# First expert weights bounded two pairs early, high part on VectorE; another order in the first pair

## The chip, the cores and the metric

The kernel runs on one core of a Trainium2 chip. The metric is the device time of one execution in microseconds (us); lower is better. On one core TensorE multiplies matrices, VectorE, ScalarE and GpSimd (POOL in the profile) work on elements, SyncE issues every load and store (SP), and 16 DMA engines carry them. TensorE writes into PSUM, which the other engines read.

## The reference

Three steps follow each other. The rows that attention gives are the rows `x` (1152 x 512) of the experts, and their sum is the input of the last step.

```
q_pool = mean of two neighbouring rows of q        # 2 batches x 8 heads, 1152 -> 576 rows, d = 64
scores = scale * q_pool @ k.T                      # 576 x 1152 a head
attn   = exp(scores - rowmax) / rowsum
x      = attn @ v                                  # gathered to 1152 x 512

p      = domain_probs / sum(domain_probs)          # 4 experts
y      = sum over e of p[:, e] * (relu(x @ w1[e]) @ w2[e])     # 512 -> 1024 -> 512

out    = ((y @ a) * (y @ b)) @ w3 @ w_out
```

## The kernel before

Every large operand is split exactly into a high and a low part, so that TensorE can work on two narrow numbers instead of a wide one: the high part is the scaled and rounded value, the low part what rounding left. To scale, the range has to be known first: a reduce over each partition, a small matmul with ones that spreads it over the partitions, and three small VectorE operations that make a power of two of it (`bounds`).

Attention goes through eight pairs of heads i = 0..7, in each two heads s, in each head nine chunks c of 128 keys. A chunk is a score product `s{i}_{s}_{c}`, two passes of ScalarE over it (exponential `p` L537, and its f16 high part `ph` L541), the low part `pl` = p - ph on GpSimd (L548) or, for the chunks named in LO_DVE and for the last pair in LAST, on VectorE (L546), and products `av` with the values `vt` (L572, L574). Beside that the next pair is prepared: keys are transposed (`kt`), their high part is made on ScalarE (`kab`) and their low part on VectorE (`kl` L263); queries are pooled on GpSimd (`QP`), transposed (`qt`) and split (`qh`, `QZ`, `ql`); `vm` (L444), `vp`, `vs` are the range of the values, and `vt` their split parts (high on ScalarE L497, low on VectorE L501). For the row maxima that the exponential subtracts, coarse score products `mp` (L367) are reduced on VectorE (`mx` L370), gathered (`mf`), turned by TensorE (`mr`) and split (`mh` on ScalarE, `ml` on VectorE L410), then laid into the operand Q2 by four small DMAs.

What runs when is an agenda: a list of (slot, function), filled with hand-written slot numbers and sorted. A pair takes 18 slots; t = 18 i. The sorted list sets the program order on each engine, and each engine works in that order. The constants at the top of the file are slots: K0, V1, VL1 for the first pair's keys and values, MX0 for the maxima, CX and CXT for the range of the rows (`cm`, `cxt`, `ca`, `cxd`, `cxs`, `cx`), W0 and WT for the weights of the experts. Score banks, `av` and two work tags (two banks and one bank) share PSUM; the work tags serve `kt`, `qt`, `mp`, `mr`, `vp`, `cxt` and `cxs` in turn, each waiting until the one before it has been read.

The clock of TensorE follows what it does, so WARM_E matmuls on an idle tile are run behind the maxima of head 0. At slot 130 the work banks are closed and three banks open for the experts: the rows are transposed (`xt` L766) and split into `xA` (high on ScalarE L783, low on VectorE L793), while the last pair still runs. The experts' weights come in 16 groups g of 256 columns. `prep_w` loads one group into two tiles `rw` of 128 x 1024, reduces them (`wm` L650), spreads and bounds them (`ws`, `wab`), and makes their high part on ScalarE (L670) and their low part on VectorE (L671). The first products `up` (L696) need `xA` and group 0.

## Time and profile before

| | us |
| --- | --- |
| median of 3 runs | 840.73 |
| runs | 839.34, 841.78, 840.73 |
| the profiled execution | 842.56 |
| its span | 840.6 |
| TensorE busy in it | 814.8 |
| VectorE, ScalarE, GpSimd busy | 602.4, 441.7, 310.6 |

The span is what the profiler saw between the first and the last instruction. A row of a timeline gives the start, the duration, the engine, the line, the operation, out<-in with shapes, how many instructions are run together (x), and in brackets the idle time of that engine before it and what ended it. Durations of matmuls that follow each other overlap.

### The profile page before, as it was taken

The page shows a single profiled execution, that of the slowest core. Times are in us where ns is not written, and L with a number is a line of the kernel's source. Part 1 is how long each engine was busy: PE and PEld are TensorE (multiplying, and loading weights), DVE is VectorE, ACT ScalarE, POOL GpSimd, SP SyncE. Part 2 cuts the span into 40 slices and gives each one's busy share as a digit, 9 for nine tenths or more (in the row PEclk, how much of TensorE's full clock was granted, in tenths as well). Part 3 has the DMA queues.
Part 4 walks back from the last instruction along what each step waited for, and adds up shares of the span by engine and source line. Part 5 has one row for each costly group of instructions (what it writes and reads, how often), then busy time and mean ns, then how long its engine had stood idle before and what let it go on. Part 6 is the DMA issues. An engine that isn't in the chain of part 4 may idle for free.

```text
span 840.6 us, 15989 instructions
## 1 busy us (share of the span) xinstructions
PE 814.8 (97%) x6367; PEld 571.4 (68%) x6367; DVE 602.4 (72%) x1025; ACT 441.7 (53%) x813; POOL 310.6 (37%) x275
## 2 busy tenths in 40 slices
PE   7789999999989999999999999999999999999998
PEld 6678889888867555555555555555556559999887
DVE  6878787887856566777788889897679778886000
ACT  2878888888775534333344445664324544433111
POOL 5788988898732000000001102221010146766100
PEclk9999999999989999999999999999999999999999
DMA  7668775774620122212232333221110222220011
GB/s 183 163 154 192 182 160 129 172 181 100 145 58 27 27 76 76 76 51 76 76 96 81 95 108 102 74 74 53 49 50 27 76 78 83 91 76 26 13 51 50
DMA packets 59834, 76.75 MB, mean 91 GB/s; under 512 B 23480, under 2 KB 41264, under 8 KB 59760
## 3 DMA queue, kind: packets, MB, share of 16 engines
q1 hardware_dynamic: 59760, 75.73, 33.9%
q8 instruction: 50, 0.82, 0.4%
q14 instruction: 24, 0.20, 0.1%
HBM read 51.92 MB, written 2.36 MB: 65 GB/s over the span
## 4 chain that ended last, share of the span: by engine, by line
PE 86%; DVE 5%; ACT 4%; DMA 2%; issue 1%; POOL 1%; SPq 0%; DVEq 0%; ACTq 0%; POOLq 0%
PE up L696 22%; PE dn L736 22%; PE gt L1210 12%; PE s L521 7%; PE o L1227 6%; PE wf L1175 5%; PE av L574 4%; PE mp L367 4%; DVE mx L370 2%; PE av L572 2%; ACT ph L541 1%; ACT p L537 1%; DMA rv<-in_v 1%; PE w3t L1162 1%; DMA Q<-qh 1%
## 5 line engine op out<-in xcount | busy, mean ns | idle before, releaser
L548 POOL TENSOR_TENSOR pl<-p,ph 128x576 f16<-128x576 f32 x131 | 169.1, 1312 | 54.9 <-ACT ph L541 50.2
L736 PE MATMUL dn<-w,h 128*128 128x512 f16 x840 | 184.7, 379 | 0.0
L696 PEld LDWEIGHTS <-w 128*128 128x128 f16 x1152 | 111.9, 98 | 77.4 <-issue 1.7
L736 PEld LDWEIGHTS <-h 128*128 128x128 f16 x840 | 81.6, 98 | 94.7
L702 ACT ACTIVATE up<-up 128x320 f32<-128x320 f32 (+1 forms) x96 | 45.7, 476 | 141.7 <-PE up L696 126.6
L370 DVE TENSOR_REDUCE mx<-mp 128x1 f32<-128x768 f32 (+1 forms) x144 | 101.9, 751 | 24.7 <-PE mp L367 24.2
L521 PE MATMUL s<-Q,K 128*128 128x288 f32 x576 | 109.9, 315 | 5.1 <-ACT ph L541 3.6
L696 PE MATMUL up<-xB,w 128*128 128x320 f16 x768 | 109.9, 299 | 0.6 <-DVE xB L793 0.5
L537 ACT ACTIVATE p<-s 128x576 f32<-128x576 f32 x131 | 84.8, 647 | 17.4 <-PE s L521 16.2
L707 DVE TENSOR_TENSOR h<-up,h 128x320 f16<-128x320 f32 (+1 forms) x94 | 51.0, 552 | 57.2 <-ACT h L703 56.9
L541 ACT ACTIVATE ph<-s 128x576 f16<-128x576 f32 x144 | 92.0, 648 | 0.0
L696 PE MATMUL up<-xA,w 128*128 128x512 f16 x384 | 90.7, 384 | 0.3 <-DVE w L671 0.3
L521 PEld LDWEIGHTS s<-Q,K 128*128 128x128 f32 x576 | 83.8, 192 | 7.1 <-ACT ph L541 4.1
L843 POOL TENSOR_TENSOR wo<-wo,cv_a 128x512 f32<-128x512 f32 x8 | 10.2, 1269 | 210.9 <-DVE wo L840 118.4
L574 PE MATMUL av<-vt,ph 128*128 128x65 f16 x720 | 80.6, 193 | 2.6 <-DVE x L584 1.5
L574 PE MATMUL av<-vt,pl 128*128 128x65 f16 x720 | 80.8, 196 | 0.0
L572 PE MATMUL av<-vt,ph 128*128 128x64 f16 x720 | 80.5, 194 | 0.0
L574 PEld LDWEIGHTS <-ph 128*128 128x128 f16 x720 | 67.1, 99 | 7.3 <-DVE x L584 3.0
L572 PEld LDWEIGHTS <-ph 128*128 128x128 f16 x720 | 66.8, 97 | 6.2 <-issue 3.3
L574 PEld LDWEIGHTS <-pl 128*128 128x128 f16 x720 | 67.0, 98 | 4.1 <-issue 1.6
L843 POOL TENSOR_TENSOR r<-r,cv_a 128x512 f32<-128x512 f32 x16 | 20.3, 1270 | 126.9 <-DVE r L840 92.1
L367 PE MATMUL mp<-kab,QZ 128*128 128x384 f32 x216 | 56.6, 369 | 1.6 <-DVE mx L370 1.3
(169 smaller groups left out, 1333.5 us busy)
## 6 DMA issues: line engine op xcount, KB each, us to landing
rw<-in_moe_w SPq DMA_DIRECT2D x64, 512.0 KB
K<-kab SPq DMA_DIRECT2D x32, 288.0 KB
rk<-in_k SPq DMA_DIRECT2D x16, 288.0 KB
rv<-in_v SPq DMA_DIRECT2D x8, 576.0 KB
Q<-qh SPq DMA_DIRECT2D x32, 144.0 KB
K<-kl SPq DMA_DIRECT2D x16, 288.0 KB
rq<-in_q SPq DMA_DIRECT2D x8, 512.0 KB
rw<-in_moe_w_out SPq DMA_DIRECT2D x8, 512.0 KB
```

The costliest lines, as they stand in the source:

```text
L367: mm(ps[:, n, :PC], QZ[:, o : o + P], KAB[i][:, sl], start=True, stop=True)
L370: nc.vector.tensor_reduce(out=mx[i, s][:, j, g : g + 1], in_=st.pop((j, g))[:, :, :PC], axis=AX.XY, op=ALU.max)
L521: mm(ps[:, n, :HALF], a[s][:, cs], b[s][:, n * HALF : (n + 1) * HALF], start=first, stop=not first,)
L537: nc.scalar.activation(out=o, in_=x, func=AF.Exp, scale=SCORE)
L541: nc.scalar.activation(out=two(o), in_=st["s"][:, :, :HALF], func=AF.Exp, scale=SCORE)
L548: nc.gpsimd.tensor_tensor(out=o, in0=st["p"], in1=h, op=ALU.subtract)
L572: mm(t[:, j, 0:D], p, vt[s][:, c, 0:D], start=False, stop=False)
L574: mm(t[:, j, :], p, vt[s][:, c, D:], start=(c == 0 and n == 0), stop=(c == NC - 1 and n == 2))
L696: mm(p, w[:, a, c, fc * P : (fc + 1) * P], x[b][:, c, lo - o : hi - o], start=(c == 0 and a == b), stop=(c == KD - 1 and a == 1),)
L707: nc.vector.tensor_tensor(out=hl[:, fc, lo:hi], in0=st["p"], in1=hh[:, fc, lo:hi], op=ALU.subtract)
L736: mm(p, hid[n][a][:, fc, t * P : (t + 1) * P], w[:, b, fc, :], start=(fc == 0 and a == b), stop=(fc == 1 and a == 1),)
L1210: mm(p, mws[n][:, m, a, c * P : (c + 1) * P], x[b][:, c, lo - o : hi - o], start=(i == 0), stop=(i == 11),)
```

## The change

Five things are changed. WARM_E goes from 27 to 45, and WARM_T adds 8 more matmuls behind the turn of head 0. In the first pair the slots K0, V1, VL1 move, Q0 and MXF are new, and so keys, queries, values and maxima stand in another order. The range of the rows (CX, CXT) is done in one go before the first maxima of pair 7's head 0 instead of between them. `prep_w` is taken apart for group 0: its load stands at slot 84 (before 123.5), its two reduces at 91.4 and 96.1, its bounds at 110.2, and its high part is made on VectorE by a tensor_scalar at 127.6 and 129.5, each followed by the low part. In the last pair chunk 4's low part goes from VectorE to GpSimd (LAST), and the split of the rows is issued later (XC).

```
--- before.py
+++ after.py
@@ -29,17 +29,18 @@
 VL0 = -4.21
 VR = 4.92
 VE = 0.35
-V1 = 4.6
-VL1 = 6.1
-K0 = 0.45
+V1 = 5.55
+VL1 = 6.3
+K0 = 1.2
+Q0 = 1.21
 L0 = (15.6, 15.7)
 LV2 = 15.8
 PQ = 1.67
 PQS = 1.3
 SH = 62.45
 XR = 120.3
-CX = 113.2
-CXT = (0, 3.4, 3.45, 5.8, 5.85)
+CX = 113.35
+CXT = (0, 0.55, 0.6, 1.25, 1.3)
 LK1 = -10
 LQ1 = -10
 LV1 = -9
@@ -48,7 +49,8 @@
 WARM = 39
 WARM_K = 10
 WARM_N = 5
-WARM_E = 27
+WARM_E = 45
+WARM_T = 8
 VH0 = 1.5
 FIRST = (0.71, 1.14, 2.3, 3.1)
 NEAR = 0.0
@@ -56,17 +58,18 @@
 KT = (3.05, 3.05)
 QT = 4.89
 MX0 = (7, 8, 10, 11.72, 13.01)
+MXF = (8, 9, 10.3, 11.72, 13.01)
 MX1 = (14, 16, 17, 18.92)
 ME = 0.07
-LAST = ((2, 4, 6), (1, 5, 7))
+LAST = ((2, 6), (1, 5, 7))
 SW = 130
-W0 = 123.5
 W1 = 134
-WT = ((0, 4.6, 8.2, 8.4, 10), (0, 7.0, 11.5, 13.0))
+WT = ((84, 91.4, 96.1, 110.2, 128.6, 127.6, 128.25, 129.5, 130.5), (0, 7.0, 11.5, 13.0))
 WN = (1, 4, 5, 3, 0)
 WS = 6
 XA = 0.0
 XS = 0.9
+XC = (0.75, 1.1)
 UA = 134
 US = 2
 DT = (139, 143.8)
@@ -419,6 +422,7 @@
         at(e, end)
         if (i, s) == (0, 0):
             at(e + TURN, turn_now)
+            at(e + TURN + 0.01, warm, WARM_T)
             return
         at(e + TURN, turn)
         at(e + TURN + 0.1, cut_hi)
@@ -629,7 +633,7 @@
 
     wab, share_of = {}, {}
 
-    def prep_w(g, space, eng=None):
+    def prep_w(g, space):
 
 
         e, o = divmod(g, PER)
@@ -644,35 +648,47 @@
                 )
                 raws.append(t)
 
-        def rows():
-            st["m"] = wtiny.tile([P, 2], BF16, tag="wm", name=f"wm{g}")
-            for m in range(2):
-                nc.vector.tensor_reduce(
-                    out=st["m"][:, m : m + 1], in_=raws[m], axis=AX.X, op=ALU.max, apply_absolute_value=True
-                )
+        def row(m):
+            if m == 0:
+                st["m"] = wtiny.tile([P, 2], BF16, tag="wm", name=f"wm{g}")
+            nc.vector.tensor_reduce(
+                out=st["m"][:, m : m + 1], in_=raws[m], axis=AX.X, op=ALU.max, apply_absolute_value=True
+            )
 
         def spread():
             p = space(f"ws{g}")
             mm(p[:, :2], ones, st["m"], start=True, stop=True)
             c = wab[g] = wtiny.tile([P, 4], F32, tag="wab", name=f"wab{g}")
             bounds(p[:, :2], c[:, 2:4], c[:, 0:2], 2.0**-100)
+
+        def share():
+            c = wab[g]
             share_of[g] = wtiny.tile([P, 9], F32, tag="sh", name=f"sh{g}")
             nc.vector.tensor_scalar(
                 out=share_of[g], in0=prx[:, :, e], scalar1=c[:, 2:3], scalar2=c[:, 3:4], op0=ALU.mult, op1=ALU.mult
             )
 
-        def cut(m):
+        def hi(m):
             if m == 0:
                 w = spl.tile([P, 2, 2, 2 * DM], F16, tag="spl", name=f"w{g}")
                 w1s[g], w2s[g] = w[:, 0], w[:, 1]
+            o, c = (w1s, w2s)[m][g][:, 0], wab[g][:, m : m + 1]
+            if g:
+                nc.scalar.activation(out=o, in_=raws[m], func=AF.Copy, scale=c)
+            else:
+                nc.vector.tensor_scalar(out=o, in0=raws[m], scalar1=c, scalar2=None, op0=ALU.mult)
+
+        def lo(m):
             w = (w1s, w2s)[m][g]
-            c = wab[g][:, m : m + 1]
-            nc.scalar.activation(out=w[:, 0], in_=raws[m], func=AF.Copy, scale=c)
-            (eng or nc.vector).scalar_tensor_tensor(
-                out=w[:, 1], in0=raws[m], scalar=c, in1=w[:, 0], op0=ALU.mult, op1=ALU.subtract
-            )
-
-        return [load, rows, spread, lambda: cut(0), lambda: cut(1)]
+            nc.vector.scalar_tensor_tensor(
+                out=w[:, 1], in0=raws[m], scalar=wab[g][:, m : m + 1], in1=w[:, 0], op0=ALU.mult, op1=ALU.subtract
+            )
+
+        steps = (load, lambda: row(0), lambda: row(1), spread, share)
+        steps += (lambda: hi(0), lambda: lo(0), lambda: hi(1), lambda: lo(1))
+        if g == 0:
+            return steps
+        return [load, lambda: run(steps[1:3]), lambda: run(steps[3:5]), lambda: run(steps[5:7]), lambda: run(steps[7:])]
 
     def up_tiles(n, space, h_tiles):
 
@@ -920,9 +936,10 @@
                 for n in range(3):
                     at(u + KT[0] - PQ + n * PQS, pool_q, i + 1, n)
                 plan_k(i + 1, u if i else u + K0)
-                plan_q(i + 1, u + QT + NEAR, u + QT + QH_)
+                q0 = 0 if i else Q0
+                plan_q(i + 1, u + QT + NEAR + q0, u + QT + QH_ + q0)
                 plan_spread(i + 1, 0, t + 9)
-                plan_max(i + 1, 0, [u + x for x in MX0])
+                plan_max(i + 1, 0, [u + x for x in (MX0 if i else MXF)])
                 plan_max(i + 1, 1, [u + x for x in MX1])
                 at((LV1, LV2)[i] if i < 2 else t + VL0, load_v, i + 1)
                 r = t + (VR if i else V1)
@@ -944,13 +961,13 @@
         later = []
 
         def plan_w(g, t, space):
-            steps = prep_w(g, space, nc.vector)
+            steps = prep_w(g, space)
             for f, d in zip(steps, WT[g]):
                 at(t + d, f)
             if g == 1:
                 later.append(steps[4])
 
-        plan_w(0, W0, one_bank)
+        plan_w(0, 0, lambda name: work(1, name)[:, 0])
         plan_w(1, W1, one_bank)
         plan_rows(CX)
         at(XR, rows_share)
@@ -961,8 +978,8 @@
         for n in range(NB):
             pe, to_hi, to_lo = rows_tile(x_src, n, one_bank, f"xt{n}", True)
             at(t + XS * n, pe)
-            at(t + XS * n + 0.2, to_hi)
-            at(t + XS * n + 0.5, to_lo)
+            at(t + XS * n + XC[0], to_hi)
+            at(t + XS * n + XC[1], to_lo)
         xb_p = []
 
         def rows_b():
```

The first pair's preparation on TensorE, before (`kt1`, `qt1`, `vp1` belong to pair 1, `mr0_1` is the turn for head 1 of pair 0):

```order
L257 MATMUL kt1_0_454<-ident_64,rk1_363 128x128 x6
L257 MATMUL kt1_1_461<-ident_64,rk1_363 128x128 x3
L521 MATMUL s0_0_4_466<-Q1_0_127,K1_0_123 128x288 x2
L521 MATMUL s0_0_4_466<-Q2_0_129,K2_0_125 128x288 x2
L310 MATMUL qt1_485<-ident_64,QP_133 128x128 x5
L448 LDWEIGHTS ones_74
L448 MATMUL vp1_491<-vm_75,ones_74 128x2
L521 MATMUL s0_0_5_497<-Q1_0_127,K1_0_123 128x288 x2
L521 MATMUL s0_0_5_497<-Q2_0_129,K2_0_125 128x288 x2
L402 MATMUL mr0_1_504<-ident_64,mf0_1_474 5x128
L521 MATMUL s0_0_6_521<-Q1_0_127,K1_0_123 128x288 x2
```

And now on TensorE in the same place of the first pair:

```order
L525 MATMUL s0_0_4_480<-Q1_0_127,K1_0_123 128x288 x2
L525 MATMUL s0_0_4_480<-Q2_0_129,K2_0_125 128x288 x2
L260 MATMUL kt1_0_492<-ident_64,rk1_390 128x128 x6
L260 MATMUL kt1_1_499<-ident_64,rk1_390 128x128 x3
L525 MATMUL s0_0_5_507<-Q1_0_127,K1_0_123 128x288 x2
L525 MATMUL s0_0_5_507<-Q2_0_129,K2_0_125 128x288 x2
L405 MATMUL mr0_1_516<-ident_64,mf0_1_486 5x128
L452 LDWEIGHTS ones_74
L452 MATMUL vp1_529<-vm_75,ones_74 128x2
L525 MATMUL s0_0_6_535<-Q1_0_127,K1_0_123 128x288 x2
L525 MATMUL s0_0_6_535<-Q2_0_129,K2_0_125 128x288 x2
L313 MATMUL qt1_543<-ident_64,QP_133 128x128 x5
```

The turn moved ahead of `vp1`, and `qt1` behind `vp1` and the chunk s0_0_6.

VectorE from the last maxima of pair 7 to the first row part, before:

```order
L370 TENSOR_REDUCE mx7_1_4314<-mp7_1_3_1_4502 128x1
L386 TENSOR_REDUCE mf7_1_4533<-mx7_1_4314 128x4
L387 TENSOR_REDUCE mf7_1_4533<-mx7_0_4118 128x1
L650 TENSOR_REDUCE wm0_4544<-rw0_0_4366 128x1
L650 TENSOR_REDUCE wm0_4544<-rw0_1_4368 128x1
L501 SCALAR_TENSOR_TENSOR vt0_121<-rv7_3693,vs7_4071,vt0_121 128x9x64
L546 TENSOR_TENSOR pl7_0_4482<-s7_0_2_4536,ph7_0_4481 128x576
L410 TENSOR_TENSOR ml7_1_4589<-mr7_1_4580,mh7_1_4584 5x128
L793 SCALAR_TENSOR_TENSOR xA1_4616<-xt0_4618,cx_77,xA0_4615 128x4x128
```

And now on VectorE in the same place:

```order
L373 TENSOR_REDUCE mx7_1_4354<-mp7_1_3_1_4538 128x1
L679 TENSOR_SCALAR w0_4562<-rw0_0_3077,wab0_3970 128x1024
L389 TENSOR_REDUCE mf7_1_4571<-mx7_1_4354 128x4
L390 TENSOR_REDUCE mf7_1_4571<-mx7_0_4170 128x1
L683 SCALAR_TENSOR_TENSOR w0_4562<-rw0_0_3077,wab0_3970,w0_4562 128x1024
L505 SCALAR_TENSOR_TENSOR vt0_121<-rv7_3727,vs7_4109,vt0_121 128x9x64
L667 TENSOR_SCALAR sh0_4599<-prx_79,wab0_3970 128x9
L550 TENSOR_TENSOR pl7_0_4518<-s7_0_2_4574,ph7_0_4517 128x576
L413 TENSOR_TENSOR ml7_1_4627<-mr7_1_4618,mh7_1_4622 5x128
L679 TENSOR_SCALAR w0_4562<-rw0_1_3079,wab0_3970 128x1024
L683 SCALAR_TENSOR_TENSOR w0_4562<-rw0_1_3079,wab0_3970,w0_4562 128x1024
L809 SCALAR_TENSOR_TENSOR xA1_4655<-xt0_4657,cx_77,xA0_4654 128x4x128
```

The two reduces `wm0` are gone from here; the high and low parts of the weights stand around `mf7_1` and `ml7_1`, all ahead of the first `xA1`.

ScalarE at the same time, from chunk 3 of pair 7's first head, before:

```order
L537 ACTIVATE p32_7_0_3_4597<-s7_0_3_4574 128x576
L541 ACTIVATE ph7_0_4481<-s7_0_3_4574 128x576
L783 ACTIVATE xA0_4615<-xt0_4618,cx_77 128x4x128
L541 ACTIVATE ph7_0_4481<-s7_0_4_4606 128x576
L537 ACTIVATE s7_0_4_4606<-s7_0_4_4606 128x2x288
L783 ACTIVATE xA0_4615<-xt1_4649,cx_77 128x4x128
L537 ACTIVATE p32_7_0_5_4679<-s7_0_5_4657 128x576
L670 ACTIVATE w0_4703<-rw0_0_4366,wab0_4688 128x1024
L783 ACTIVATE xA0_4615<-xt2_4697,cx_77 128x4x128
```

And now on ScalarE in the same place:

```order
L541 ACTIVATE p32_7_0_3_4635<-s7_0_3_4612 128x576
L545 ACTIVATE ph7_0_4517<-s7_0_3_4612 128x576
L541 ACTIVATE p32_7_0_4_4675<-s7_0_4_4645 128x576
L799 ACTIVATE xA0_4654<-xt0_4657,cx_77 128x4x128
L545 ACTIVATE ph7_0_4517<-s7_0_4_4645 128x576
L541 ACTIVATE p32_7_0_5_4718<-s7_0_5_4697 128x576
L799 ACTIVATE xA0_4654<-xt1_4689,cx_77 128x4x128
L545 ACTIVATE ph7_0_4517<-s7_0_5_4697 128x576
L545 ACTIVATE ph7_0_4517<-s7_0_6_4736 128x576
```

The two weight parts are gone, and each row part `xA0` stands behind the exponential of the next chunk.

## Rows read from the trace of the kernel before

**Rows 1.** The page, busy time by engine: us (share of the span) xinstructions

```profile
PE 814.8 (97%) x6367; PEld 571.4 (68%) x6367; DVE 602.4 (72%) x1025; ACT 441.7 (53%) x813; POOL 310.6 (37%) x275
```

**Rows 2.** Timeline of TensorE, first pair (columns as told above)

```profile
14.49 1.68 PE L874 MATMUL warm<-idle 128*128 128x128 f16 x27
17.56 0.70 PE L397 MATMUL mr<-ident,MT 128*2 128x128 f32 x5 [1.39 <-DVE MT L391]
...
30.41 0.73 PE L310 MATMUL qt<-ident,QP 128*128 128x128 f32 x5 [1.13 <-DVE kl L263]
32.05 0.18 PE L448 MATMUL vp<-vm,ones 128*128 128x2 bf16 x1 [0.90 <-DVE vm L444]
...
34.40 0.79 PE L521 MATMUL s<-Q,K 128*128 128x288 f32 x4 [0.90 <-ACT ph L541]
35.03 0.69 PE L367 MATMUL mp<-kab,QZ 128*128 128x384 f32 x3
```

**Rows 3.** Windows: from:to, us; busy PE, PEld, DVE, ACT, POOL; PEclk, DMA share, GB/s

```profile
20.00:25.00 5.00, 4.95 (x21) 4.43 (x21) 3.29 (x5) 4.03 (x7) 2.91 (x3) 0.66 0.91 274
...
30.00:35.00 5.00, 2.79 (x19) 2.31 (x20) 4.33 (x9) 3.90 (x9) 2.58 (x4) 1.00 0.10 27
...
235.00:240.00 5.00, 2.12 (x20) 1.93 (x20) 3.53 (x5) 5.00 (x9) 1.29 (x1) 0.84 0.33 105
240.00:245.00 5.00, 5.00 (x25) 2.78 (x25) 2.25 (x5) 2.54 (x5) 3.07 (x2) 0.50 0.42 105
```

**Rows 4.** Timeline of VectorE, first pair

```profile
26.56 1.41 DVE L370 TENSOR_REDUCE mx<-mp 128x1 f32<-128x768 f32 x2
...
29.31 1.42 DVE L263 TENSOR_TENSOR kl<-kt,kab 128x768 fp32r<-128x768 f32 x2 [1.08 <-ACT kab L260]
30.65 1.34 DVE L444 TENSOR_REDUCE vm<-rv 128x2 bf16<-128x1152 f32 x1
...
33.30 0.28 DVE L410 TENSOR_TENSOR ml<-mr,mh 5x128 f32<-5x128 f32 x1 [0.30 <-ACT mh L406]
```

**Rows 5.** Timeline of VectorE, pairs 5 and 6

```profile
167.80 0.98 DVE L501 SCALAR_TENSOR_TENSOR vt<-rv,vs,vt 128x576 f16<-128x576 f32 x1
...
176.33 1.42 DVE L370 TENSOR_REDUCE mx<-mp 128x1 f32<-128x768 f32 x2 [1.17 <-PE mp L367]
...
182.03 1.71 DVE L501 SCALAR_TENSOR_TENSOR vt<-rv,vs,vt 128x576 f16<-128x576 f32 x1
```

**Rows 6.** Timeline of TensorE, pairs 5 and 6

```profile
170.01 0.55 PE L257 MATMUL kt<-ident,rk 128*128 128x128 f32 x3 [0.18 <-DVE ml L410]
...
207.88 0.27 PE L469 MATMUL cxt<-ident,cm 128*2 128x128 f32 x1 [0.91 <-DVE mx L370]
```

**Rows 7.** Timeline of TensorE, end stage

```profile
236.60 0.78 PE L521 MATMUL s<-Q,K 128*128 128x288 f32 x4 [1.66 <-ACT ph L541]
...
239.05 1.33 PE L521 MATMUL s<-Q,K 128*128 128x288 f32 x4 [1.28 <-DVE pl L546]
```

**Rows 8.** Timeline of VectorE, end stage

```profile
225.84 2.34 DVE L650 TENSOR_REDUCE wm<-rw 128x1 bf16<-128x1024 f32 x2
228.09 0.81 DVE L501 SCALAR_TENSOR_TENSOR vt<-rv,vs,vt 128x576 f16<-128x576 f32 x1
...
235.47 1.28 DVE L671 SCALAR_TENSOR_TENSOR w<-rw,wab,w 128x1024 f16<-128x1024 f32 x1 [1.03 <-ACT w L670]
```

**Rows 9.** Timeline of ScalarE, end stage

```profile
230.56 0.69 ACT L783 ACTIVATE xA<-xt,cx 128x512 f16<-128x512 f32 x1 [1.99 <-PE xt L766]
...
234.28 1.15 ACT L670 ACTIVATE w<-rw,wab 128x1024 f16<-128x1024 f32 x1 [0.82 <-DVE wab L436]
```

**Rows 10.** Line L830: count, duration ns min/median/max, first and last start

```profile
L830 DVE TENSOR_SCALAR cv_a<-cv_a x40: 407/419/1389, 350.5 to 762.9; 128x512 f32<-128x512 f32 x40
```

**Rows 11.** Windows around the new load (columns as in rows 3)

```profile
160.00:161.00 1.00, 1.00 (x16) 0.94 (x15) 0.28 (x1) 0.64 (x2) 1.00 (x1) 1.00 0.00 0
```

**Rows 12.** Timeline of TensorE, first score of pair 5

```profile
164.70 0.76 PE L521 MATMUL s<-Q,K 128*128 128x288 f32 x4
```

More of the change, by code (lines that the diff above doesn't have):

```diff
@@ L31 @@
 VE = 0.35
-V1 = 4.6
-VL1 = 6.1
-K0 = 0.45
+V1 = 5.55
+VL1 = 6.3
+K0 = 1.2
+Q0 = 1.21
 L0 = (15.6, 15.7)
@@ L40 @@
 XR = 120.3
-CX = 113.2
-CXT = (0, 3.4, 3.45, 5.8, 5.85)
+CX = 113.35
+CXT = (0, 0.55, 0.6, 1.25, 1.3)
 LK1 = -10
@@ L50 @@
 WARM_N = 5
-WARM_E = 27
+WARM_E = 45
+WARM_T = 8
 VH0 = 1.5
@@ L69 @@
 XS = 0.9
+XC = (0.75, 1.1)
 UA = 134
@@ L421, in plan_max @@
             at(e + TURN, turn_now)
+            at(e + TURN + 0.01, warm, WARM_T)
             return
@@ L645, in load, with row @@
                 raws.append(t)
-        def rows():
-            st["m"] = wtiny.tile([P, 2], BF16, tag="wm", name=f"wm{g}")
-            for m in range(2):
-                nc.vector.tensor_reduce(
-                    out=st["m"][:, m : m + 1], in_=raws[m], axis=AX.X, op=ALU.max, apply_absolute_value=True
-                )
+        def row(m):
+            if m == 0:
+                st["m"] = wtiny.tile([P, 2], BF16, tag="wm", name=f"wm{g}")
+            nc.vector.tensor_reduce(
+                out=st["m"][:, m : m + 1], in_=raws[m], axis=AX.X, op=ALU.max, apply_absolute_value=True
+            )
         def spread():
@@ L667, in cut, with lo @@
                 w1s[g], w2s[g] = w[:, 0], w[:, 1]
+            o, c = (w1s, w2s)[m][g][:, 0], wab[g][:, m : m + 1]
+            if g:
+                nc.scalar.activation(out=o, in_=raws[m], func=AF.Copy, scale=c)
+            else:
+                nc.vector.tensor_scalar(out=o, in0=raws[m], scalar1=c, scalar2=None, op0=ALU.mult)
+        def lo(m):
             w = (w1s, w2s)[m][g]
-            c = wab[g][:, m : m + 1]
-            nc.scalar.activation(out=w[:, 0], in_=raws[m], func=AF.Copy, scale=c)
-            (eng or nc.vector).scalar_tensor_tensor(
-                out=w[:, 1], in0=raws[m], scalar=c, in1=w[:, 0], op0=ALU.mult, op1=ALU.subtract
-            )
-        return [load, rows, spread, lambda: cut(0), lambda: cut(1)]
+            nc.vector.scalar_tensor_tensor(
+                out=w[:, 1], in0=raws[m], scalar=wab[g][:, m : m + 1], in1=w[:, 0], op0=ALU.mult, op1=ALU.subtract
+            )
+        steps = (load, lambda: row(0), lambda: row(1), spread, share)
+        steps += (lambda: hi(0), lambda: lo(0), lambda: hi(1), lambda: lo(1))
+        if g == 0:
+            return steps
+        return [load, lambda: run(steps[1:3]), lambda: run(steps[3:5]), lambda: run(steps[5:7]), lambda: run(steps[7:])]
     def up_tiles(n, space, h_tiles):
@@ L922, in tile_kernel @@
                 plan_k(i + 1, u if i else u + K0)
-                plan_q(i + 1, u + QT + NEAR, u + QT + QH_)
+                q0 = 0 if i else Q0
+                plan_q(i + 1, u + QT + NEAR + q0, u + QT + QH_ + q0)
                 plan_spread(i + 1, 0, t + 9)
-                plan_max(i + 1, 0, [u + x for x in MX0])
+                plan_max(i + 1, 0, [u + x for x in (MX0 if i else MXF)])
                 plan_max(i + 1, 1, [u + x for x in MX1])
@@ L946, in plan_w @@
         def plan_w(g, t, space):
-            steps = prep_w(g, space, nc.vector)
+            steps = prep_w(g, space)
             for f, d in zip(steps, WT[g]):
@@ L951, in plan_w @@
                 later.append(steps[4])
-        plan_w(0, W0, one_bank)
+        plan_w(0, 0, lambda name: work(1, name)[:, 0])
         plan_w(1, W1, one_bank)
```

16 lines of the change are left out of this document (9 added, 7 removed).

## The prediction

> **What bounds the kernel now.** I read the page first: TensorE is busy for 97% of the span [rows 1], so only its idle time and its slow stretches can be won, and nothing the other engines save counts unless it ends one of those. The idle time before each TensorE instruction came next, along its timeline; it lies in two places that the change touches, the preparation of pair 1 behind the first scores [rows 2] and the passage from the last pair to the experts [rows 7]. Each row there names in brackets how long TensorE stood and who released it. Then the table by windows, for the granted clock [rows 3]: 0.66 of full in 20 to 25 us and 0.50 in 240 to 245 us, which is the lower of the two levels (1.2 GHz), against 1.00 elsewhere. Before each fall TensorE had stood: for 1.39 us before the `mr` at 17.56 [rows 2], and with 2.12 us of work in all of 235 to 240. The stretch 30 to 35 us has 2.79 and kept its clock, so a gap does not always cost the clock. Behind these places, through most of each pair, TensorE has no gap, so a shift in pair 0 is not absorbed: it moves the end.
>
> **First pair: the warm matmuls.** 18 more behind the maxima of head 0 and 8 behind the turn, at 1.68/27 = 0.062 us each [rows 2], are 1.1 and 0.5 us of work. The first lie in the idle 1.39 us before the `mr` at 17.56 [rows 2], the others while TensorE waits for the `vm` behind it, so they cost nothing. If they hold the clock at 2.4 GHz from 20 on, the maxima products, 0.69 us at the high clock [rows 2] and up to twice that at half of it, no longer delay VectorE's reduces: over the first two of head 1 some 0.4 and 0.3 us, so that the last pair of reduces starts at 25.86 and not at 26.56 [rows 4]. Gain at the head of the chain: 0.7 us.
>
> **First pair: the order.** Replayed from rows. The keys' transposes follow these reduces as before; their low part on VectorE ends at 30.73 - 0.7 = 30.03 [rows 4]. The row turn `mr` of head 1 now stands before `vp` and the second half of the scores; it needs the PSUM bank that this low part frees, so it runs at 30.15. Its high part on ScalarE and the low part `ml` on VectorE (0.28 us [rows 4]) end at about 31.0. Only then can the value maximum run (1.34 us [rows 4]), to 32.35, where it ended at 31.99 before; `vp` follows at 32.35 against 32.05 [rows 2]. TensorE is in order, and the query transposes now stand behind `vp` and s0_0_6: they start at 33.0 instead of 30.41 [rows 2]. That is 2.6 us later. From there to the first maxima product of pair 1 lay 4.6 us (35.03 [rows 2]); in the replay 3.7 remain, since fewer score chunks are left ahead of it on ScalarE; so it comes at about 36.7. Scores go on meanwhile (s0_0_7 at about 33.5 instead of 34.40 [rows 2], whose wait of 0.90 goes), so some idle time is filled. But what follows is paced by maxima steps with 1.4 us of reduces each [rows 4], and the same set of instructions ends 1.5 us later, the 0.7 already taken off. Bounds: -0.7, if the scores that move forward fill all of the new gap; +3.5, if the stretch from 28.5 to 32.35, where only one score chunk (0.6 us) and one `mr` (0.25) are left to run, costs the clock for the next 4 us. I take +1.5, nearer the row that kept its clock (30 to 35 us).
>
> **Early range of the expert weights.** Two reduces of 1.17 us (2.34 for both [rows 8]) leave the end stage. The second stands before mx6_0_0, where VectorE is idle for 1.17 us [rows 5]: nothing. The first stands between the last maxima of pair 5 and `mf`: there the chain mf, `vt` low, `pl`, `ml` releases the key transposes, which wait 0.18 us already [rows 6]. 1.17 us more stand in front of it; the low `vt` part behind it took 0.98 us there [rows 5] and 0.81 in the end stage [rows 8], so up to 0.2 may come back. Cost 0.9 us; 1.75 at most, if it falls against a long POOL instruction as the 1.71 us one did [rows 5]; 0 at least, if the reduces before it end early. The three operations on the bounds stand in the same place one pair later; each is of the size of an `ml` or smaller (0.28 [rows 4]), so 0.2 to 0.8; I take 0.4. The transfer itself (1 MB) moves on SP's queue to before the shifts of pair 5 and the values of pair 6. At 160 us the DMA engines have run empty [rows 11]; 1 MB more at the 274 GB/s of 20 to 25 us [rows 3] is 3.8 us of traffic in front of shifts that are wanted by the score at 164.70 [rows 12]: 0, at most 1.0, since the queue was empty for some of it.
>
> **Range of the rows, `cx`.** The wait of 0.91 us at `cxt` [rows 6] goes. In its place `cxt` and `cxs` wait ahead of the next score chunks for four and two small operations on VectorE; I replayed about 0.65 and 0.95 us there, in which scores and `av` catch up by the old place: 0, plus or minus 0.4.
>
> **The end stage.** ScalarE before: the high part of chunk 4 waited behind xA, which itself waited 1.99 us for `xt0` [rows 9]; now the exponential of chunk 4 goes before xA and its high part right behind. The two weight parts of 1.15 us each leave ScalarE [rows 9]; the one at 234.28 stands right ahead of the chain that released s7_0_7 after 1.66 us idle [rows 7]. On VectorE the two reduces (2.34) go from the place ahead of the low `vt`, and a high part by tensor_scalar over 128 x 1024 (0.82, twice the 0.419 us median of the 128 x 512 row [rows 10]) plus the low part (1.28 [rows 8]) come in: 2.10 against 2.34, so `ml`, and with it the row transposes `xt0` that wait for its bank, stay within 0.2 us of where they were. Replayed without any collision, s7_0_7 goes from 236.60 to 234.8 and s7_0_8 from 239.05 [rows 7] to 236.8: 2.25 us. Behind it TensorE is full, at the low clock for all of 240 to 245 [rows 3]; if the shorter gaps keep the clock, 5.0 x 0.5 = 2.5 us more, 4.8 in sum. With collisions: the high and low part each wait for a POOL product that has begun (1.29 us each [rows 3]), `xt0` comes 1.6 us later, s7_0_8 at about 238.1, and the clock falls as before: gain 1.0. Chunk 4's low part on POOL instead of VectorE stays hidden: POOL is busy for 1.29 of the 5 us from 235 [rows 3]. I take 3.4: between the ends, nearer the upper, since half of the clock's loss returns even in a middling case.
>
> A row for the collision: the same low `vt` instruction takes 0.81 us where POOL is idle [rows 8] and 1.71 where POOL runs back to back [rows 5]; the copy of [rows 10] ranges from 0.407 to 1.389. The Trainium skill, page "SBUF — State Buffer", section "SBUF: two separate sides", says that a VectorE instruction in a two-port mode or with two SBUF inputs and a GpSimd instruction take one port pair as a lock, the loser waiting for the whole instruction. The page "VectorE: DVE Perf Modes" (section on the tier table) has an fp32 tensor_scalar in SBUF in that class. By that rule both new weight parts queue against POOL, which speaks against the change; the rows agree as far as `vt` goes, and no row shows the high part itself. By it the sum would be rival 3's, without it the one below.
>
> **The sum.** +1.5 + 0.9 + 0.4 + 0 + 0 - 3.4 = -0.6 us. The profiled execution took 842.56 us (span 840.6) [rows 1] and stands 1.8 above the median of 840.73; against the median that is 840.1.
>
> **The rivals.** (1) *The order in pair 0 is free and the end gives all.* For it: two of the four waits in [rows 2] are waits that the new order steps around, and the clock row shows what is to be had. Against it: the query chain of 2.6 us. -0.7 + 0.9 + 0.4 - 4.8 = -4.2: 836.5. (2) *Slower: the clock falls in pair 0.* With 0.85 us of work in the 3.85 us from 28.5, TensorE is emptier there than in 235 to 240 (2.12 of 5 [rows 3]), in which the clock did fall. It decides if the clock goes under 1.0 between 30 and 35 us. +3.5, the first reduce at its upper 1.75, +0.55, the end stage at 1.8: +4.0, so 844.7. Against it: 30 to 35 us as it is now kept its clock with 2.79 [rows 3]. (3) *VectorE and POOL block each other in the end stage*, so that the early weights bring nothing there but the clock's fall as before: 1.5 + 0.9 + 0.4 - 1.0 = +1.8, 842.5; the change then doesn't do what it says.
>
> **How the numbers follow.** A measurement of this kernel can tell about 0.3%, 2.5 us, from no change. Forecast 0.35 (0.34 within, 0.01 faster); rival 1 0.32, faster; rival 2 0.20, slower; rival 3 0.13 (0.11 within, 0.02 slower). So faster 0.33, same 0.45, slower 0.22. The range reaches to both outer rivals, 836.3 to 844.5; what lies past them is the far half of each, together under 0.2.
>
> **What would show it.** In the changed profile: the clock row of 20 to 25 us at 1.00 (the warm matmuls); the query transposes at about 33 us and the first maxima product of pair 1 behind 36 us (the order), with the clock row of 30 to 35 us for rival 2; the key transposes of pair 6 waiting about 1 us for `ml`; the wait of 0.91 at `cxt` gone; the score chunks 7 and 8 of pair 7 at about 235 and 237 and the clock row of 240 to 245 at 1.00. If the query transposes come where they were, the first pair's term is wrong; if the high part takes over 1.2 us or starts late behind a POOL product, rival 3 is right.

## The result

The changed kernel took 848.76 us (median of 7 runs, 845.77 to 851.3) against 841.78 for the kernel before (7 runs, 839.34 to 845.54): ratio 1.0082, 95% interval 1.0056 to 1.0107, slower by 7 us. The forecast was 840.1, and the time lies above the top of the range. The profiled execution has a span of 846.1 us against 840.6, so 5.5 us are to be found in the two traces.

They are found by following the same instruction through both. The first column of numbers is the start in the kernel before, the second in the changed one.

| instruction | before | changed | behind by |
| --- | --- | --- | --- |
| second key transposes of pair 2, first pair over | 56.40 | 58.26 | 1.86 |
| `av` behind the shares of the experts, pair 3 | 125.43 | 128.48 | 3.05 |
| second key transposes of pair 6 | 170.01 | 174.63 | 4.62 |
| `av` of the following head | 180.60 | 186.79 | 6.19 |
| second key transposes of pair 7 | 198.42 | 204.98 | 6.56 |
| last `av` that waits before the end stage | 210.42 | 217.09 | 6.67 |
| score chunk 8 of pair 7, head 0 | 239.05 | 247.40 | 8.35 |
| end of the span | 840.6 | 846.1 | 5.5 |

So the loss has six parts: 1.9 us in the first pair, 1.2 at the shares in pair 3, 1.6 at the key transposes of pair 6, 1.6 right behind them, 0.5 from the bounds and the row range, 1.7 in the end stage up to score chunk 8. Behind that chunk 2.85 come back. The last two are one stretch: from the last `av` that waits to the end it is 630.2 us before and 629.0 now, 1.2 less.

TensorE in the first pair of the changed kernel, to be read beside [rows 2]:

```profile
17.34 0.71 PE L400 MATMUL mr<-ident,MT 128*2 128x128 f32 x5 [0.38 <-DVE MT L394]
...
29.60 0.28 PE L405 MATMUL mr<-ident,mf 128*5 128x128 f32 x1 [1.49 <-DVE kl L266]
31.79 0.16 PE L452 MATMUL vp<-vm,ones 128*128 128x2 bf16 x1 [1.92 <-DVE vm L448]
...
32.92 1.27 PE L313 MATMUL qt<-ident,QP 128*128 128x128 f32 x5
...
37.16 0.68 PE L370 MATMUL mp<-kab,QZ 128*128 128x384 f32 x3
```

The query transposes come at 32.92 (30.41 before), and before the turn and before the spread of the value range TensorE stands 1.49 and 1.92 us for VectorE. The windows of the changed kernel (from:to and length in us, busy PE, PEld, DVE, ACT, POOL with counts, the granted clock, DMA share, GB/s), beside [rows 3]:

```profile
20.00:25.00 5.00, 4.20 (x23) 2.99 (x21) 4.47 (x7) 4.48 (x9) 3.41 (x4) 1.00 0.97 247
...
30.00:35.00 5.00, 3.21 (x14) 2.99 (x13) 3.01 (x6) 2.01 (x5) 1.66 (x3) 0.66 0.24 55
...
175.00:180.00 5.00, 5.00 (x70) 4.71 (x69) 2.30 (x4) 3.22 (x6) 2.59 (x3) 0.68 0.56 117
...
235.00:240.00 5.00, 1.96 (x26) 1.75 (x27) 4.96 (x7) 1.62 (x3) 1.46 (x1) 0.96 0.16 35
240.00:245.00 5.00, 5.00 (x59) 4.71 (x57) 2.08 (x3) 2.82 (x6) 1.78 (x2) 0.70 0.55 158
```

One window of the kernel before that [rows 3] does not have:

```profile
175.00:180.00 5.00, 5.00 (x54) 4.29 (x50) 3.52 (x8) 4.68 (x10) 4.85 (x5) 1.00 0.95 240
```

The clock of 20 to 25 us is now 1.00, as the warm matmuls were to bring, but 30 to 35 us fell from 1.00 to 0.66; 175 to 180, which had kept its clock before, has 0.68, and 240 to 245 has 0.70 instead of 0.50. The last two numbers stand for different work: in the kernel before, score chunk 8 starts at 239.05 and the low window lies behind it; in the changed kernel it starts at 247.40 and the low window lies ahead of it.

The first reduce of the weights and the low value part behind it on VectorE, and TensorE's waits in pairs 6 and 7, beside [rows 5, 6]:

```profile
170.66 1.22 DVE L654 TENSOR_REDUCE wm<-rw 128x1 bf16<-128x1024 f32 x1
...
171.93 1.78 DVE L505 SCALAR_TENSOR_TENSOR vt<-rv,vs,vt 128x576 f16<-128x576 f32 x1
```

```profile
174.63 0.80 PE L260 MATMUL kt<-ident,rk 128*128 128x128 f32 x3 [1.64 <-DVE ml L413]
...
204.98 0.55 PE L260 MATMUL kt<-ident,rk 128*128 128x128 f32 x3 [0.51 <-DVE ml L413]
...
209.55 0.27 PE L473 MATMUL cxt<-ident,cm 128*2 128x128 f32 x1 [0.38 <-DVE cm L467]
...
211.55 0.16 PE L485 MATMUL cxs<-cxd,ones 128*128 128x2 bf16 x1 [0.91 <-DVE cxd L479]
```

The low value part took 1.78 us where [rows 5] had 0.98, and the key transposes stood 1.64 us instead of 0.18. One pair on, with three small operations in front instead of the reduce, it is 0.51. The wait of 0.91 us at `cxt` became one of 0.38 there and 0.91 at `cxs`.

VectorE in the end stage, beside [rows 8], GpSimd at the same time, TensorE, beside [rows 7], and the first row transpose of the kernel before:

```profile
232.58 1.06 DVE L679 TENSOR_SCALAR w<-rw,wab 128x1024 f16<-128x1024 f32 x1
...
233.70 2.17 DVE L683 SCALAR_TENSOR_TENSOR w<-rw,wab,w 128x1024 f16<-128x1024 f32 x1
235.79 1.83 DVE L505 SCALAR_TENSOR_TENSOR vt<-rv,vs,vt 128x576 f16<-128x576 f32 x1
...
238.61 0.73 DVE L679 TENSOR_SCALAR w<-rw,wab 128x1024 f16<-128x1024 f32 x1
239.38 1.28 DVE L683 SCALAR_TENSOR_TENSOR w<-rw,wab,w 128x1024 f16<-128x1024 f32 x1
```

```profile
231.81 2.98 POOL L552 TENSOR_TENSOR pl<-p,ph 128x576 f16<-128x576 f32 x2 [0.99 <-ACT ph L545]
235.55 1.46 POOL L552 TENSOR_TENSOR pl<-p,ph 128x576 f16<-128x576 f32 x1 [0.76 <-ACT ph L545]
```

```profile
238.83 0.63 PE L782 MATMUL xt<-ident,x 128*128 128x128 f32 x4 [2.52 <-DVE ml L413]
...
247.40 0.80 PE L525 MATMUL s<-Q,K 128*128 128x288 f32 x4 [1.01 <-DVE pl L550]
```

```profile
229.90 0.63 PE L766 MATMUL xt<-ident,x 128*128 128x128 f32 x4 [0.48 <-DVE ml L410]
```

The high part of the first weight tile takes 1.06 us while GpSimd works and that of the second 0.73 while it does not; the low parts take 2.17 and 1.28; the low value part takes 1.83 where [rows 8] has 0.81. TensorE stood 2.52 us at the first row transpose instead of 0.48 before.

One loss lies at a place that the change does not touch. Four small operations make the experts' shares, once, before a division that frees `av`'s bank in pair 3. The last of them, GpSimd's instruction beside it, and TensorE behind it, in the kernel before and then in the changed one:

```profile
124.29 0.20 DVE L898 TENSOR_TENSOR pr<-pr_raw,pr_s 128x36 f32<-128x36 f32 x1
```

```profile
124.28 2.57 POOL L548 TENSOR_TENSOR pl<-p,ph 128x576 f16<-128x576 f32 x2 [0.31 <-ACT ph L541]
```

```profile
125.43 0.20 PE L574 MATMUL av<-vt,ph 128*128 128x65 f16 x1 [1.46 <-DVE x L584]
```

```profile
126.23 1.30 DVE L914 TENSOR_TENSOR pr<-pr_raw,pr_s 128x36 f32<-128x36 f32 x1
```

```profile
126.21 2.51 POOL L552 TENSOR_TENSOR pl<-p,ph 128x576 f16<-128x576 f32 x2 [0.29 <-ACT ph L545]
```

```profile
128.48 0.20 PE L578 MATMUL av<-vt,ph 128*128 128x65 f16 x1 [2.60 <-DVE x L588]
```

The same 128 x 36 operation took 0.20 and 1.30 us, and TensorE's wait grew from 1.46 to 2.60. In the changed kernel the operation ended about when the first of two GpSimd subtractions did, which had started 0.02 us ahead of it. In the kernel before it met the same pair of subtractions, 0.01 us behind, and went through. In all eleven profiles that have the shares at this place the two start within 0.02 us of each other; in five VectorE takes 0.20, in six 1.30 to 1.32. So the collision is always there, and which of the two goes first turns on hundredths of a us. GpSimd went first in five of the six profiles that have both the new order and the added warm matmuls, and in one of the five others; whether the change decides it is not shown.

### The profile page after: what moved, and what is told of

Same layout as the page of the kernel before. It is cut to its first block, busy times and chain, and to the rows that moved or that the text cites. A ratio compares the mean times of both kernels' runs of the same rounds, so it can differ in the third digit from the quotient of the medians.

```text
span 846.1 us, 16044 instructions
## 1 busy us (share of the span) xinstructions
PE 815.8 (96%) x6393; PEld 573.1 (68%) x6393; DVE 607.7 (72%) x1026; ACT 440.1 (52%) x811; POOL 311.4 (37%) x276
## 4 chain that ended last, share of the span: by engine, by line
PE 86%; DVE 7%; ACT 3%; DMA 2%; issue 1%; SPq 0%; POOL 0%; DVEq 0%; ACTq 0%
PE up L712 22%; PE dn L752 22%; PE gt L1227 12%; PE s L525 6%; PE o L1244 6%; PE wf L1192 5%; PE av L578 4%; PE mp L370 4%; DVE mx L373 3%; PE av L576 2%; ACT ph L545 1%; DMA rv<-in_v 1%; ACT p L541 1%; PE w3t L1179 1%; DVE vt L505 1%
## 5 line engine op out<-in xcount | busy, mean ns | idle before, releaser
L712 PE MATMUL up<-xA,w 128*128 128x512 f16 x384 | 89.0, 379 | 0.3 <-DVE w L683 0.3
```

What stands on the lines that cost most here:

```text
L712: mm(p, w[:, a, c, fc * P : (fc + 1) * P], x[b][:, c, lo - o : hi - o], start=(c == 0 and a == b), stop=(c == KD - 1 and a == 1),)
```

## The experiments

Theory after the two traces: **(A)** the new order of the first pair lengthens its chain and costs the clock behind it; **(L)** VectorE instructions that read two operands from SBUF, the on-chip memory of the operands, and the copy-like ones, such as the tensor_scalar, wait while GpSimd's subtraction runs, so that what the change puts on VectorE costs more than its length where GpSimd works: at the first reduce's place and in the end stage. The rivals are in the expectations. Each ratio is to the kernel before on the same chip; the changed kernel's is 1.0082. A difference between two ratios carries both intervals, which makes it uncertain by nearly 3 us either way (an estimate from the intervals).

**The first pair's old order in the changed kernel.**

```
-V1, VL1, K0, Q0 = 5.55, 6.3, 1.2, 1.21
-MXF = (8, 9, 10.3, 11.72, 13.01)
+V1, VL1, K0, Q0 = 4.6, 6.1, 0.45, 0
+MXF = (7, 8, 10, 11.72, 13.01)
```

> The changed kernel with the first pair's old order (slots of keys, queries, values and maxima as before), the longer warm stretch kept. Theory A: the new order costs 1.9 us by the place where TensorE runs full again (kt of pair 2 at 58.26 against 56.40) and it is the order that makes the clock fall in 30 to 35 us; this kernel is then 2 to 3 us faster than the changed one, about 846, and its clock row of 30 to 35 us is 1.00. Rival: the added warm matmuls bring the clock fall forward; then this kernel stays at about 848.5 and the clock still falls before 40 us.

843.81 us, ratio 1.0023 (1.0002 to 1.0043): some 5 us better than the changed kernel, more than expected. The second key transposes of pair 2 start at 56.61 in place of 58.26, 1.65 us earlier, near the 1.9 that A named. The rest lies behind and is not the order's: the shares' operation went ahead of GpSimd (0.20 us, TensorE's wait 1.46), and the clock of 175 to 180 stayed at 1.00 though the wait at the key transposes was the same (1.63). The clock of 30 to 40 us was not at 1.00 (0.88 and 0.78), so the old order does not keep it for certain either: that part of A fell.

**The new order alone.** The kernel before with the edit above reversed.

> The kernel before with the new order of the first pair alone, without the added warm matmuls. Theory A: 2 to 3 us slower than before, about 844, the loss complete by 60 us. Rival (the order is harmless, other parts of the change cost): within 1 us of before.

844.54 us, ratio 1.0034 (1.0012 to 1.0056): 2.9 us slower, as A said, and in its profile the second key transposes of pair 2 come at 59.66, 3.26 later than before. Its windows:

```profile
30.00:35.00 5.00, 2.38 (x13) 2.21 (x14) 3.67 (x8) 1.64 (x5) 2.56 (x2) 0.85 0.20 49
35.00:40.00 5.00, 3.62 (x15) 3.27 (x13) 1.63 (x2) 4.60 (x9) 3.50 (x5) 0.50 0.20 41
```

The clock fell to its lower level for all of 35 to 40 us.

**The warm matmuls alone.**

```
-WARM_E = 27
+WARM_E = 45
+WARM_T = 8
+            at(e + TURN + 0.01, warm, WARM_T)
```

> The kernel before with the 18 + 8 added warm matmuls alone. My forecast for the changed kernel had this part at -0.7 us: 841, the clock row of 20 to 25 us at 1.00. Rival: the time gained at the head of the chain is taken back before the first pair is full: 841.8, no change. If the warm matmuls hurt: over 842.5.

841.11 us, ratio 0.9995 (0.9975 to 1.0014): no difference. The gain at the head is there (first key transposes at 26.68 instead of 27.57), and the second key transposes of pair 2 come 0.9 us earlier; but at the shares GpSimd went first, and the clock fell behind the wait of 2.59 us that followed. Two of those operations and the window behind them:

```profile
122.28 0.76 DVE L896 TENSOR_SCALAR pr_s<-pr_s 128x9 f32<-128x9 f32 x1
...
123.32 1.31 DVE L900 TENSOR_TENSOR pr<-pr_raw,pr_s 128x36 f32<-128x36 f32 x1
```

```profile
125.00:130.00 5.00, 4.42 (x46) 4.13 (x46) 3.97 (x6) 1.71 (x3) 2.10 (x2) 0.66 0.86 226
```

**The reduces in VectorE's idle stretches.**

```
-WT = ((84, 91.4, 96.1, 110.2, ...
+WT = ((66, 78.1, 96.1, 110.2, ...
```

> The changed kernel with the expert weights loaded one pair earlier still and the first reduce moved out of the chain before the turn of pair 5, into VectorE's idle stretch before the first maxima of pair 5. Theory: the reduce costs 1.6 us of TensorE's wait at the key transposes (174.63) and some 1.5 more by the clock that falls behind it; this kernel is about 3 us faster, 845.5, and the clock row of 175 to 180 is 1.00. Rival: the load's new place on the queue is what costs (it stands earlier here, before the shifts of another pair): no gain, 848.5 or more, with a wait for a DMA in the trace.

844.76 us, ratio 1.0036 (1.0017 to 1.0056): some 4 us better than the changed kernel. The low value part of pair 5 with nothing in front, the one reduce that is left there, and TensorE at the key transposes:

```profile
171.86 0.99 DVE L505 SCALAR_TENSOR_TENSOR vt<-rv,vs,vt 128x576 f16<-128x576 f32 x1
...
179.13 1.21 DVE L654 TENSOR_REDUCE wm<-rw 128x1 bf16<-128x1024 f32 x1
```

```profile
174.06 0.55 PE L260 MATMUL kt<-ident,rk 128*128 128x128 f32 x3 [0.17 <-DVE ml L413]
```

The wait is back to 0.17 us and the clock of 175 to 180 us at 1.00. That the wait had pulled the clock down is not shown by this: in four other kernels, above and below, that leave the reduce in place the wait is 1.63 or 1.64 us, and behind it the clock stayed at 1.00 in three (the old order, the split behind the chain, the high parts on ScalarE) and fell in one (0.78, GpSimd out of the way). The load, now earlier still, made no wait for a DMA there: the rival fell.

**The weights' split behind the chain to the row transposes.**

```
-... 110.2, 128.6, 127.6, 128.25, 129.5, 130.5), ...
+... 110.2, 129.42, 129.4, 129.41, 133.85, 133.9), ...
```

> The changed kernel with the split of the first weights behind the chain that releases the row transposes: the high and low part of the first tile after ml of pair 7, those of the second after the last row part. Nothing else differs. Theory L: in the changed kernel the two weight parts before the low values (1.06 and 2.17 us) and the stretched low values (1.83) hold ml back, and TensorE stands 2.52 us for it and loses its clock; without them ml comes over 3 us earlier, the wait at the first row transpose is under 1 us and the kernel is 2.5 to 4 us faster, about 845.5. Rival: the row parts, now behind the weights, become the bound and score chunks 7 and 8 come no earlier: 848.

843.01 us, ratio 0.9998 (0.9976 to 1.002): about 7 us better than the changed kernel, more than the 2.5 to 4 expected, and level with the kernel before, with the other losses still in. VectorE and TensorE in its end stage:

```profile
233.19 0.98 DVE L505 SCALAR_TENSOR_TENSOR vt<-rv,vs,vt 128x576 f16<-128x576 f32 x1
...
236.04 2.33 DVE L683 SCALAR_TENSOR_TENSOR w<-rw,wab,w 128x1024 f16<-128x1024 f32 x1
238.29 1.25 DVE L667 TENSOR_SCALAR sh<-prx,wab 128x9 f32<-128x9 f32 x1
```

```profile
235.85 0.60 PE L782 MATMUL xt<-ident,x 128*128 128x128 f32 x4
...
242.81 0.80 PE L525 MATMUL s<-Q,K 128*128 128x288 f32 x4 [0.85 <-DVE pl L550]
```

The first row transpose no longer waits. From the last waiting `av` to score chunk 8 it is 25.2 us (242.81 - 217.57), in the changed kernel 30.3 and before 28.6; so this trace shows 5.1 us of the gain. The low part still took 2.33 us and the small share 1.25 against GpSimd; behind the chain they cost TensorE no wait that the stretch shows.

**The high parts on ScalarE**, in the order of that kernel: the activation in place of the tensor_scalar, the first at slot 130.05.

> As the kernel with the weights behind the chain, but with the high parts on ScalarE (the first in the 2 us that ScalarE stands idle before the first row part, the second late). Theory L: VectorE has 0.73 us less in front of the first row part; the same as that kernel or up to 0.7 us faster, about 845. Rival: ScalarE is what the score chunks wait for, and 1.15 us in front of chunk 4 delays them: 1 us slower than that kernel.

844.07 us, ratio 1.0007 (0.9986 to 1.0028), the stretch again 25.25 us (246.12 - 220.87). So it makes no difference that can be told here which engine makes the high part.

**GpSimd out of the way.**

```
-                    nc.gpsimd.tensor_tensor(out=o, in0=st["p"], in1=h, op=ALU.subtract)
+                    if i == 7 and s == 0 and c < 4:
+                        nc.gpsimd.memset(o, 0.0)
+                    else:
+                        nc.gpsimd.tensor_tensor(out=o, in0=st["p"], in1=h, op=ALU.subtract)
```

> The changed kernel with GpSimd's three low parts of pair 7, head 0, chunks 0, 1 and 3 replaced by a zero fill of the same tile: it leaves out the low part of these chunks' weights, so its time has 3 GpSimd subtractions less and is otherwise the changed kernel's. Theory L (VectorE's instructions with two operands in SBUF wait while GpSimd reads): the high part takes 0.73 instead of 1.06, the low part 1.28 instead of 2.17, the low values 0.81 instead of 1.83; ml 2.2 us earlier, the kernel 2 to 3 us faster, about 846. Rival (these instructions are long for themselves, by size or operands): durations as in the changed kernel, 848.5.

845.3 us, ratio 1.0016 (0.9999 to 1.0034), some 5 us better than the changed kernel. VectorE at the place where the changed kernel has 1.06, 2.17 and 1.83, and TensorE at the first row transpose:

```profile
235.58 0.75 DVE L682 TENSOR_SCALAR w<-rw,wab 128x1024 f16<-128x1024 f32 x1
...
236.38 1.27 DVE L686 SCALAR_TENSOR_TENSOR w<-rw,wab,w 128x1024 f16<-128x1024 f32 x1
237.57 0.81 DVE L505 SCALAR_TENSOR_TENSOR vt<-rv,vs,vt 128x576 f16<-128x576 f32 x1
```

```profile
239.58 0.63 PE L785 MATMUL xt<-ident,x 128*128 128x128 f32 x4 [0.27 <-DVE ml L413]
```

The three durations are those that L named, and TensorE's wait is 0.27 instead of 2.52. The order of VectorE's and TensorE's instructions is the changed kernel's; only GpSimd's three subtractions are gone. The fills in their place, 1.62 us from 233.76, were over before the first of the three operations began. So it is shown that GpSimd's work lengthens these operations; that it is its reading of SBUF, as L has it, and no other part of the work, is not shown here. The stretch to score chunk 8 is 26.4 us (246.57 - 220.13), 2.2 less than before: what the prediction's replay without any collision had (2.25).

**TensorE's gaps in the first pair filled.**

```
+        at(5.1, warm, 20)
+        at(5.85, warm, 28)
```

> The changed kernel with 20 + 28 more warm matmuls (0.062 us each) in TensorE's two waits of the first pair, 1.49 us before the turn and 1.92 us before the spread of the value range; they take no time from anything. Theory C: the new order's loss is half the clock's, which falls in 30 to 40 us because TensorE stands; with the waits filled the clock row of 30 to 40 us is 1.00 and the kernel 1.5 to 3 us faster than the changed one, about 846. Rival: the loss is the chain's length alone; the clock stays up and the time is the changed kernel's, 848.5.

847.5 us, ratio 1.0059 (1.0046 to 1.0072): lower than the changed kernel's 1.0082, but the intervals overlap. In its profile the gaps and the clock behind them:

```profile
29.86 0.27 PE L405 MATMUL mr<-ident,mf 128*5 128x128 f32 x1 [0.37 <-DVE kl L266]
...
32.05 0.16 PE L452 MATMUL vp<-vm,ones 128*128 128x2 bf16 x1 [0.35 <-DVE vm L448]
```

```profile
30.00:35.00 5.00, 3.57 (x43) 3.21 (x41) 3.38 (x7) 2.90 (x6) 2.71 (x4) 1.00 0.27 63
35.00:40.00 5.00, 3.83 (x24) 3.07 (x24) 3.21 (x5) 5.00 (x10) 4.13 (x4) 1.00 0.51 106
```

The clock stayed at 1.00, and the first maxima product of pair 1 came at 36.37 instead of 37.16, still 1.3 later than the 35.03 of [rows 2]. So between these two profiles 0.8 us of the delay is the clock's. In this one the turn stands 0.26 us later already (29.86 instead of 29.60); counted from the turn the clock's part is 1.05 us of the 2.1, half, as theory C had it. The profile of the changed kernel got off lightly: in those with the reduces moved, the high parts on ScalarE and GpSimd out of the way, which have the same first pair, the clock of 35 to 40 us is 0.50, and from the turn to the second key transposes of pair 2 it is 29.8 to 30.1 us instead of 28.7. There the clock's part is 2 us or a little more (an estimate: 1.05 and the 1.1 to 1.4 us of difference).

**The shares elsewhere** (`SH = 62.45` to 42.1, nothing else, in the kernel before).

> The kernel before with four small VectorE operations (the shares of the experts, once per run) moved from before av's division in pair 3 to an idle stretch before the maxima of pair 3. Theory L: there they met GpSimd by chance (one of them 1.30 us in the changed kernel's profile, 0.20 in that of before) and TensorE waited 1.46 us in one case and 2.6 in the other; now it waits under 0.3 and the kernel is 1.0 to 2.5 us faster than before, 840. Rival: the four operations run into the chain of the maxima there and give the time back: 841.5.

842.77 us, ratio 1.0003 (0.9983 to 1.0022): the rival. The wait at `av` went, and one of 1.28 us at a maxima product of pair 3 came: the four operations met GpSimd at the new place as well (1.25 and 0.98 us for two of them).

**The repaired kernel**: the first pair's old order, the reduces in idle stretches and the split behind the chain, that is, the first, fourth and fifth edit together.

> The changed kernel with three edits taken back or moved at once: the first pair's old order, both reduces of the weights in VectorE's idle stretches (loaded one pair earlier), and the weights' split behind ml of pair 7. What is left of the change: the longer warm stretch, the early range, the row range in one go, the high part on VectorE, the later row parts. Theory: 0.7 (warm) and 3 to 4 us (the end stage 25.2 us long instead of 28.6 from the last wait of av to score chunk 8) come off the kernel before, less 0.4 for the bounds: 838.5, ratio 0.996. Rival: the gains of the parts don't add, since time won in front is taken back by the row shares' wait near 125 us: 841.

839.2 us, ratio 0.9960 (0.9939 to 0.9981): the ratio that was expected. **With the shares and the bounds moved too** (SH = 42.1; load, reduces and bounds at 48, 60.1, 78.1 and 96.15):

> The repaired kernel with the shares in an idle stretch as well, the weights loaded another pair earlier and their bounds in VectorE's idle stretch of pair 6, so that nothing of them stands before a turn. Theory: 1.5 to 2.5 us below the repaired kernel, 836.5, ratio 0.994. Rival: the shares' and bounds' new places delay the maxima: as the repaired kernel.

838.94 us, ratio 0.9958 (0.9946 to 0.997): as the repaired kernel, which was the rival, with a wait of 1.29 us at the maxima product again. **With the shares at the start instead** (the repaired kernel with SH = 0.0):

> The repaired kernel with the four small operations on the shares at the start, where VectorE waits for the first maxima products of head 1 and GpSimd has nothing to do yet, instead of before av's division in pair 3. Theory L: alone they take under 1.2 us together (two of them 0.74 and 0.2 to 1.3 against GpSimd elsewhere), TensorE's wait of 1.45 us near 126 us goes, and at most 0.5 us is lost at the head of the first chain: about 1 us below the repaired kernel, ratio to before 0.995. Rival: the first chain is delayed by all of it: as the repaired kernel, 0.996 or above.

835.62 us (6 runs, 834.79 to 836.59), ratio 0.9898 (0.9862 to 0.9933): the best kernel of this study, about 1% below the kernel before. That is more than the 0.995 expected, and not all of it is the move's: the kernel before took 844.4 us on this chip and 842.24 on that of the repaired kernel, and the spans of the two profiles differ by 1.6 us (834.5 and 836.1). The four operations where GpSimd has nothing to do:

```profile
20.18 0.19 DVE L908 TENSOR_REDUCE pr_s<-pr_raw 128x9 f32<-128x36 f32 x1
20.41 0.17 DVE L910 TENSOR_SCALAR pr_s<-pr_s 128x9 f32<-128x9 f32 x1
20.61 0.21 DVE L913 RECIPROCAL pr_s<-pr_s 128x9 f32<-128x9 f32 x1
20.86 0.20 DVE L914 TENSOR_TENSOR pr<-pr_raw,pr_s 128x36 f32<-128x36 f32 x1
```

0.78 us together, where the kernel before spends 1.33 on them; TensorE waits no longer at `av` in pair 3, and no window of 5 us between 40 and 280 us is below full clock.

## Why the prediction was wrong

The sum of -0.6 us stands against 5.5 us between the two profiles. The step that failed most is the end stage: the sum took 3.4 us of gain there, and its collision of VectorE with GpSimd was sized with one wait where there were three. The first reduce cost 2.2 us more than its term, counting the low clock behind it, and the shares' 1.2 us were not in the sum. By the steps of the prediction:

- *Warm matmuls, -0.7.* Right and a little small: the last reduces of head 1 start at 25.38 (forecast 25.86). As the only edit they make no difference that can be told (ratio 0.9995); in that profile the 0.9 us won in front are lost again at the shares.
- *Order of the first pair, +1.5.* 1.86 in the traces, with the warm matmuls' gain taken off as in the forecast; 2.9 us as the only edit, where the forecast without that gain is 2.2 (1.5 + 0.7). The replay's landmarks held: query transposes 32.92 (33.0), spread 31.79 (32.35), first maxima product 37.16 (36.7). The clock fell, as rival 2 had it: at about 1 us in the profile of the changed kernel, and at rival 2's 2 or a little more in three other profiles of the same first pair.
- *First reduce, +0.9, at most 1.75.* The wait grew by 1.46, inside the bounds. What failed was the choice between them: the 0.98 of [rows 5] already held some waiting for GpSimd, and behind the reduce it became 1.78, which is [rows 5]'s 1.71 again. And the bound left the clock out: it fell right behind the wait in this profile, 1.6 us more. Of the four other profiles with the same wait three kept the clock.
- *Bounds, +0.4; the load, 0; the row range, 0.* About 0.4 measured for the bounds (the wait at the key transposes went from 0.17 to 0.51); no wait for a DMA at the first score of pair 5; waits of 0.38, 0.91 and 0.32 at the row range in place of 0.91 and 0.50 us, 0.2 more.
- *End stage, -3.4.* The step that failed. To score chunk 8 the stretch became 1.7 us longer instead of 1.0 to 2.25 shorter, outside both bounds. The mechanism was in the text, as the collision and as rival 3, but the collision was sized with one wait of 1.6 us in all. Three instructions in a row each waited: 0.33, 0.89 and 1.02 us over their lengths alone, 2.24 together. And the chain that released the row transposes stood behind all of them, because the high and low part had been put ahead of `ml`, so TensorE's wait there grew from 0.27 us without GpSimd's subtractions to 2.52 with them. Behind that wait the clock fell, ahead of score chunk 8 (0.70 in 240 to 245 us). Without the subtractions the stretch is 26.4 us, so the replay without a collision was right. That GpSimd's subtractions are the cause is shown by that kernel: 0.75, 1.27 and 0.81 us. The size of the high part alone, put at 0.82 us (twice 0.419 is 0.84), is 0.73 to 0.75. The Trainium skill, page "SBUF — State Buffer", section "SBUF: two separate sides", has a rule for this: a VectorE instruction with two inputs in SBUF, or in a mode that uses two ports, and a GpSimd instruction share one pair of ports as a lock, and whichever starts first keeps it for its whole instruction. These durations agree with it.
- *The clock's return behind it, 2.5 us.* From score chunk 8 to the end it is 598.7 us in the changed kernel and 601.6 before. But the kernel with the warm matmuls alone has the old end stage and 598.7 too, and two more profiles with the old end stage have 600.0 and 600.3: what one profile shows there, 2.9 us, is not a price. And in the changed kernel the loss had only moved ahead of chunk 8. In the four profiles with its end stage as it is, it takes 628.7 to 629.0 us from the last waiting `av` to the end; in the four with the old end stage 627.3 to 630.2, in the mean 628.8; in the five with the weights' split behind the chain 623.9. So where 3.4 us were to be won, nothing was, and 5 us were there to be had.
- *Not in the sum*: the shares' operation (1.2 us), which no edit of the change touches; whether the change or chance decided who went first there is open.

How the parts add is only partly settled. Three edits taken back one at a time win 5, 4 and 7 us, together more than the change lost; each of these numbers is uncertain by nearly 3 us, and each kernel also took its own turn at the shares and with the clock. The profiled sums above are of one execution each, while the ratios are of medians.

## What to carry over

An element operation of the kinds seen here that is moved to VectorE is priced by what GpSimd runs at that moment, not by its length alone, and so is the instruction behind it; put it where nobody waits on VectorE's queue, or where GpSimd is idle. Ahead of a small operation that releases TensorE, nothing long may stand. A loss or gain of clock seen in one execution is not a term of a sum: look at more executions with the same stage.
